# Casting q and early k in the loading DMA, bundling the attention work of a step, a two-input mask and layer-norm applies on VectorE, in a fused sliding-window attention and gMLP kernel

## The chip, the cores and the metric

One core of one Trainium2 chip runs the kernel. The metric is the device time of one execution in microseconds (us). Engines are named as in the profile: PE is TensorE, PEld its weight loads, DVE is VectorE, ACT is ScalarE, POOL is GpSimd, SP is SyncE. "L311" is line 311 of the kernel file of that run.

## The reference, cut to what matters

```python
# attention: 8 batches, 8 heads, 576 positions, head size 64, window of 64 positions
scores = scale * q @ k.transpose(0, 1, 3, 2)
mask = (rel >= 0) & (rel < 64)               # rel = query position - key position
attn = softmax(where(mask, scores, -1e9))
x = (attn @ v) -> [8, 576, 512]              # heads side by side

# gMLP on x
h = relu(x @ w_in);  u, v = h[..., :512], h[..., 512:]
v_n = (v - mean(v)) / sqrt(var(v) + 1e-6)    # layer norm without gain
v_s = einsum('ts,bsd->btd', w_spatial, v_n) + b_spatial[None, :, None]
out = (u * v_s) @ w_out                      # float32
```

## The kernel before

Each batch's attention is five steps: four pairs of heads, and one step for the last 64 positions of all heads. A step has these pieces: T (transposes of q and k on TensorE, then a copy `qk` on VectorE), S (scores), E (exponential on ScalarE, then the mask on VectorE), P (a product with ones for the softmax sums, then the products with v), N1 (logarithm of the sums) and N2 (reciprocal, then VectorE's `x`). The gMLP of the batch before supplies products V, U, G and O. `oz`, the PSUM tile of P, has one buffer, so the P of a step waits until VectorE has made `x` of the step before. The gMLP products share three PSUM buffers called `mm`.

```python
# loads: f32, by hardware queues; q, and k of the first three batches, in 1 KB runs
def load_runs(b, x, h0, n, eng):
    eng.dma_start(NAT[b][x] ... [:, h0:h0 + n, :],
                  SRC[x][b, h0:h0 + n, 0:512, :].rearrange("h (p j) d -> p h (j d)", j=4))

# casts to f16: one per tensor and head pair, on GpSimd (batch 0: k on ScalarE, q on VectorE)
steps.append([lambda p=p: cast_pair(b, 1, p, engk), lambda p=p: cast_pair(b, 0, p, engq),
              lambda p=p: cast_pair(b, 2, p, nc.gpsimd), lambda p=p: shift_pair(b, p, nc.gpsimd)])

# T: 8 transposes of 128 columns; E: the mask
for c in range(4):
    nc.tensor.transpose(tp[:, 128 * c:128 * c + 128], Qh[:, c, 2 * s:2 * s + 2, :], id16[:, :])
nc.vector.scalar_tensor_tensor(e2[:, :, :], e2[:, :, :], 0.0, m, ALU.max, ALU.min)

# layer norm of batch b
nc.vector.scalar_tensor_tensor(nb[:, :], mv[:, :, 0], -1.0, rs[:, :], ALU.mult, ALU.mult)
for j in range(5):
    ...
    (nc.vector if b < 1 else nc.gpsimd).tensor_scalar(
        vn[0:jn, :], vs[0:jn, :], rs[0:jn, j:j + 1], nb[0:jn, j:j + 1], ALU.mult, ALU.add)

# one step: gMLP products (todo) are put between the pieces
def att_step(i, s, todo, before, between, nxt):
    if nxt is not None:
        emit_T(*nxt)
    run(todo, before)
    post = []
    if i < B:
        emit_S(i, s)
        post.append(lambda: emit_E(i, s))
    if state["P"] is not None:
        pb, ps_ = state["P"]
        emit_P(pb, ps_)
        post.append(lambda: emit_N1(pb, ps_))
        post.append(lambda: emit_N2(pb, ps_))
    while post:
        post.pop(0)()
        run(todo, between)
    state["P"] = (i, s) if i < B else None
```

The softmax here doesn't subtract the row's maximum and nothing guards it: scores larger than these inputs give would overflow.

## Time and profile before

The median is 262.28 us (261.06 to 264.21, three runs); in the profiled execution the span is 259.1 us. Busy time of each engine, from the top of the profile page, and engines' shares of the chain of waits that ended last:

```profile
PE 220.0 (85%) x2586; PEld 117.0 (45%) x2586; DVE 165.8 (64%) x298; ACT 152.3 (59%) x272; POOL 172.8 (67%) x275
...
PE 52%; POOL 12%; DVE 12%; ACT 12%; DMA 5%; issue 5%; ACTq 1%; POOLq 0%; SPq 0%
```

TensorE is the busiest, but half of the chain runs through other engines. The next rows cut the span at three products: the first V product, the second batch's fourth U product (U4, where the chain of waits enters it), and the same product five batches later. A row gives the window, its length, the busy time of PE, PEld, DVE, ACT and POOL (with instruction counts), the granted TensorE clock, the busy share of the DMA queues (packets overlap, so it can exceed 1) and GB/s. The last row is one steady batch.

```profile
0.00:32.00 32.00, 23.49 (x251) 11.91 (x251) 19.49 (x49) 13.23 (x22) 25.09 (x46) 0.89 1.10 230
32.00:91.56 59.56, 45.82 (x506) 24.96 (x502) 39.44 (x69) 32.75 (x58) 45.06 (x80) 0.86 1.02 233
91.56:223.90 132.34, 121.20 (x1571) 66.01 (x1570) 93.39 (x155) 89.26 (x160) 98.84 (x147) 1.00 0.49 127
223.90:259.10 35.20, 29.50 (x266) 14.13 (x263) 13.50 (x26) 17.09 (x32) 3.77 (x5) 1.00 0.19 68
...
145.70:171.86 26.16, 24.25 (x316) 13.24 (x314) 18.87 (x31) 17.84 (x32) 22.06 (x34) 1.00 0.73 182
```

In the first two rows, 91.56 us, TensorE is idle for 22 us (91.56 − 23.49 − 45.82) and the clock is below full. In a steady batch it is idle for 1.9 of 26.16 us. The timeline of TensorE shows where. Its columns are the start, the duration, the instruction, and in brackets the idle time before it with what ended it:

```profile
165.88 0.41 PE L311 MATMUL oz_1_3167<-e_5_1_3067,onesK 128*64 128x512 f16 x2 [1.07 <-DVE x_0_3101 L339]
...
170.72 0.39 PE L430 MATMUL ps_0_3240<-wspT_153,vn_3_3137 128*128 128x512 f16 x1 [0.36 <-POOL vn_3_3137 L400]
171.47 0.39 PE L430 MATMUL ps_0_3240<-wspT_154,vn_0_137 65*128 65x512 f16 x1 [0.36 <-POOL vn_0_137 L400]
```

The ones product waits for `x`, and the first G product waits for layer-norm outputs that GpSimd makes one after another. Before the steady state, four waits stand out in the list of waits of 45 to 93 us (total, times, longest):

```profile
POOL hv_784 L119 <- DMA nv_608<-in_v_dram: 7.7, 1, 7.7
...
PE oz_3_1198 L311 <- DVE x_2_1159 L339: 6.0, 1, 6.0
PEld L238 <- POOL hk_783 L119: 4.5, 1, 4.5
...
ACT ob_3_1152 L455 <- DMA out_dram<-ob_0_1059: 3.3, 1, 3.3
```

ScalarE stands 3.3 us before an output copy because an output buffer is still being stored, and TensorE's 6.0 us follow.

### The profile page before, as it was taken

Reading aid. Unit: us, or ns where it says so; the run is one execution under the profiler, and the core shown is the slowest. Engines: PE = TensorE matmul, PEld = TensorE weight load, DVE = VectorE, ACT = ScalarE, POOL = GpSimd, SP = SyncE. Lnnn points to the kernel's source line nnn. Section 1 sums busy time; section 2 is a strip of 40 time slices with the busy share of each in tenths; the row PEclk is TensorE's granted clock in tenths of the full one; section 3 lists DMA queues with packets and bytes.
Section 4 is the critical chain, followed back from the end, with each engine's and each line's share of the span. In section 5 each row is a group of like instructions: output and inputs, shape, how many; then the busy total and the mean of one; then the engine's idle time right before and its main releaser. Section 6 shows DMA issues by size and latency. Waiting matters only on the chain.

```text
span 259.1 us, 6474 instructions
## 1 busy us (share of the span) xinstructions
PE 220.0 (85%) x2586; PEld 117.0 (45%) x2586; DVE 165.8 (64%) x298; ACT 152.3 (59%) x272; POOL 172.8 (67%) x275
## 2 busy tenths in 40 slices
PE   8577895899097899868998899889988998899892
PEld 2344452455054355534554455446543654354350
DVE  2866676485389556964878387838783878376130
ACT  3344575147357646774588558855885488657422
POOL 2799979129979995969688968897789402400500
PEclk9959999599779799999999999999999999999999
DMA  7999999999999809990587858680220023002304
GB/s 194 293 220 242 210 262 243 237 204 259 256 223 253 184 4 226 265 240 3 121 238 199 177 123 227 194 193 0 83 101 4 3 81 105 1 3 81 104 11 171
DMA packets 85310, 40.41 MB, mean 156 GB/s; under 512 B 68192, under 2 KB 80032, under 8 KB 85280
## 3 DMA queue, kind: packets, MB, share of 16 engines
q1 hardware_dynamic: 80448, 34.87, 56.1%
q0 software_dynamic: 1408, 2.24, 4.6%
q10 hardware_dynamic: 3424, 2.88, 3.5%
q8 instruction: 20, 0.33, 0.5%
q14 instruction: 10, 0.08, 0.1%
HBM read 32.79 MB, written 9.44 MB: 163 GB/s over the span
## 4 chain that ended last, share of the span: by engine, by line
PE 52%; POOL 12%; DVE 12%; ACT 12%; DMA 5%; issue 5%; ACTq 1%; POOLq 0%; SPq 0%
DMA out_dram<-ob_0_1059 3%; DMA nq_78<-in_q_dram 2%; POOL vn_1_138 L400 1%; DMA out_dram<-ob_1_4740 1%; POOL vn_0_137 L400 1%; PE ps_0_810 L430 1%; DVE maskr L194 1%; PE warm_304 L158 1%; POOL vn_1_2013 L400 1%; PE pv_0_1260 L364 1%; POOL vn_1_4201 L400 1%; POOL vn_1_3679 L400 1%; POOL vn_1_3133 L400 1%; POOL vn_1_2573 L400 1%; POOL vn_0_1460 L400 1%
## 5 line engine op out<-in xcount | busy, mean ns | idle before, releaser
L311 PEld LDWEIGHTS <-onesK 128*64 128x64 f16 x80 | 6.0, 107 | 19.5 <-issue 16.9
L400 POOL TENSOR_SCALAR vn_0_4595<-vs_0_4520,rs_4590,nb_4591 128x512 f16<-128x512 f16 x1 | 0.8, 773 | 17.3 <-PE pu_0_4613 L410 17.3
L400 POOL TENSOR_SCALAR vn_0_4199<-vs_0_4051,rs_4194,nb_4195 128x512 f16<-128x512 f16 x1 | 0.8, 772 | 14.7 <-DVE nb_4195 L392 14.7
L119 POOL CAST hv_102<-nv_80 128x512 f16<-128x512 f32 (+1 forms) x5 | 5.0, 997 | 5.4 <-DMA nv_80<-in_v_dram 5.3
L158 PEld LDWEIGHTS <-scratch 128*128 128x128 f16 x49 | 5.0, 117 | 7.3 <-issue 4.1
L119 POOL CAST hv_784<-nv_608 128x512 f16<-128x512 f32 (+1 forms) x5 | 3.1, 613 | 7.7 <-DMA nv_608<-in_v_dram 7.7
L158 PE MATMUL warm_105<-scratch 128*128 128x512 f16 x14 | 5.9, 616 | 1.3 <-DVE scratch L153 1.3
L119 POOL CAST hq_782<-nq_606 128x256 f16<-128x256 f32 (+1 forms) x9 | 4.6, 533 | 2.3 <-DMA nq_606<-in_q_dram 2.3
L119 POOL CAST hk_1232<-nk_794 128x512 f16<-128x512 f32 (+1 forms) x5 | 5.7, 1131 | 0.2
L311 PE MATMUL oz_3_1198<-e_1_3_1143,onesK 128*64 128x512 f16 x2 | 0.6, 608 | 6.0 <-DVE x_2_1159 L339 6.0
L294 ACT ACTIVATE e_1_0_837<-sc_0_819 128x1024 f16<-128x1024 f32 x1 | 1.0, 1024 | 7.6 <-PE sc_0_819 L273 7.6
L137 POOL COPY hs_1761<-hv_1760 64x512 f16<-64x512 f16 x4 | 3.3, 828 | 3.0 <-PE oz_4_1822 L324 2.8
L117 ACT CAST hk_101<-nk_79 128x256 f16<-128x256 f32 x8 | 2.8, 400 | 3.9 <-DMA nk_79<-in_k_dram 3.9
L410 PEld LDWEIGHTS <-win_141 128*128 128x128 f16 x32 | 3.2, 101 | 4.1 <-issue 0.6
L410 PEld LDWEIGHTS <-win_142 128*128 128x128 f16 x32 | 3.2, 101 | 4.1 <-issue 0.6
L119 POOL CAST hk_2319<-nk_1763 128x512 f16<-128x512 f32 (+1 forms) x5 | 4.8, 961 | 0.2
L119 POOL CAST hk_3439<-nk_2883 128x512 f16<-128x512 f32 (+1 forms) x5 | 4.8, 961 | 0.2
L119 POOL CAST hk_2879<-nk_2323 128x512 f16<-128x512 f32 (+1 forms) x5 | 4.8, 961 | 0.2
L119 POOL CAST hk_417<-nk_421 128x256 f16<-128x256 f32 (+1 forms) x9 | 4.5, 527 | 0.3
L119 DVE CAST hq_100<-nq_78 128x256 f16<-128x256 f32 x8 | 2.1, 300 | 4.0 <-DMA nq_78<-in_q_dram 4.0
L119 POOL CAST hq_1758<-nq_1235 128x256 f16<-128x256 f32 (+1 forms) x9 | 4.6, 531 | 0.0
L410 PEld LDWEIGHTS <-win_140 128*128 128x128 f16 x32 | 3.3, 102 | 2.9 <-issue 0.3
(1869 smaller groups left out, 1000.7 us busy)
## 6 DMA issues: line engine op xcount, KB each, us to landing
nv_422<-in_v_dram SPq DMA_DIRECT2D x9, 128.0 KB, 5.0
nk_79<-in_k_dram SPq DMA_DIRECT2D x4, 256.0 KB, 4.9
nq_78<-in_q_dram SPq DMA_DIRECT2D x4, 256.0 KB, 4.8
nk_421<-in_k_dram SPq DMA_DIRECT2D x4, 256.0 KB, 8.2
nq_420<-in_q_dram SPq DMA_DIRECT2D x4, 256.0 KB, 8.7
nk_607<-in_k_dram SPq DMA_DIRECT2D x2, 512.0 KB, 5.8
nq_606<-in_q_dram SPq DMA_DIRECT2D x2, 512.0 KB, 8.6
nv_608<-in_v_dram SPq DMA_DIRECT2D x4, 256.0 KB, 7.3
```

What stands on the lines that cost most here:

```text
L117: nc.scalar.copy(o, i)
L119: eng.tensor_copy(o, i)
L137: eng.tensor_copy(vs[0:64, 0:4, hs, :], vn[0:64, 0:4, hs, :])
L158: nc.tensor.matmul(t[:, :], scratch[:, 0:128], scratch[:, :], start=True, stop=True)
L194: nc.vector.tensor_scalar(maskr[:, u, :], keep[:], -1.0, BIG, ALU.mult, ALU.add)
L294: nc.scalar.activation(e2[:, :, :], sc[:, :, :], AF.Exp, bias=0.0, scale=0.125)
L311: nc.tensor.matmul(oz[64 * h:64 * h + 64, 1, 0:n], onesK[:, :], e2[:, h, 0:n], start=True, stop=True)
L364: nc.tensor.matmul(pv[:, :], X[b, r][:, 128 * j:128 * j + 128], w_in_sb[r][:, 512:1024], start=(r == 0), stop=(r == 3))
L400: (nc.vector if b < 1 else nc.gpsimd).tensor_scalar(vn[0:jn, :], vs[0:jn, :], rs[0:jn, j:j + 1], nb[0:jn, j:j + 1], ALU.mult, ALU.add)
L410: nc.tensor.matmul(pu[:, :], w_in_sb[r][:, 128 * m:128 * m + 128], X[b, r][:, :], start=(r == 0), stop=(r == 3))
L430: nc.tensor.matmul(ps[:, :], VN[b, kk][0:kn, 128 * m:128 * m + 128], wspT[kk][0:kn, 0:512], start=(kk == 0), stop=(kk == 4))
```

## The change

The intent is to take work off GpSimd and to take the two steady waits away. It has these parts.

1. **Loads.** q, and k of the first three batches, are loaded by GpSimd's DMA queue, which casts to f16 on the way. Their casts go, and q's f32 tiles. The v shift copies read f32.
2. **Half-width transposes.** The casting loads leave each head's 1 KB run together, so q and early k are transposed 64 columns at a time: sixteen instead of eight transposes.
3. **Mask.** A two-input `min` in place of `max` then `min`.
4. **Bundle.** P, S, N1, T, E, N2 of a step are issued together, and its gMLP products after them.
5. **Layer-norm applies** of all batches on VectorE, as subtract then multiply.
6. **Output buffers**: five instead of three, all stores by SyncE.

```diff
-    def load_runs(b, x, h0, n, eng):
-        eng.dma_start(NAT[b][x][:, 0:4, :, :] ...
+    def load_runs(b, x, h0, n):
+        nc.gpsimd.dma_start(runs(b, x)[:, h0:h0 + n, :, :].rearrange("p h j d -> p h (j d)"),
+                            SRC[x][b, h0:h0 + n, 0:512, :].rearrange("h (p j) d -> p h (j d)", j=4))
 # ... (start of the program: six of ten casting loads here, the mask source "keep" after all ten)
+    for p in (2, 3):
+        for x in (1, 0):
+            load_runs(0, x, 2 * p, 2)
+    for x in (1, 0):
+        load_runs_rem(0, x)
 # ... (emit_T)
+                    for j in range(4):
+                        for h in (0, 1):
+                            nc.tensor.transpose(tp[64 * h:64 * h + 64, o + 128 * j:o + 128 * j + 128],
+                                                src[:, 2 * s + h, j, :], id16[:, :])
 # ... (emit_E)
-        nc.vector.scalar_tensor_tensor(e2[:, :, :], e2[:, :, :], 0.0, m, ALU.max, ALU.min)
+        nc.vector.tensor_tensor(e2[:, :, :], e2[:, :, :], m, ALU.min)
 # ... (emit_LN)
-            (nc.vector if b < 1 else nc.gpsimd).tensor_scalar(
-                vn[0:jn, :], vs[0:jn, :], rs[0:jn, j:j + 1], nb[0:jn, j:j + 1], ALU.mult, ALU.add)
+            nc.vector.tensor_scalar(vn[0:jn, :], vs[0:jn, :], mv[0:jn, j, 0:1],
+                                    rs[0:jn, j:j + 1], ALU.subtract, ALU.mult)
 # ... (outputs)
-        ob = mpool.tile([128, 512], f32, tag="ob", bufs=3, name=f"ob{b}_{j}")
+        ob = mpool.tile([128, 512], f32, tag="ob", bufs=5, name=f"ob{b}_{j}")
 # ... (one step)
-    def att_step(i, s, todo, before, between, nxt):
+    def att_step(i, s, nxt):
+        if state["P"] is not None:
+            emit_P(*state["P"])
+        if i < B:
+            emit_S(i, s)
+        if state["P"] is not None:
+            emit_N1(*state["P"])
         if nxt is not None:
             emit_T(*nxt)
-        # ... interleaved pieces and products
+        if i < B:
+            emit_E(i, s)
+        if state["P"] is not None:
+            emit_N2(*state["P"])
         state["P"] = (i, s) if i < B else None
 # ... (second batch)
-        att_step(1, s, todo, 1, 1 if s else 0, (1, s + 1) if s < 4 else (2, 0))
+        att_step(1, s, (1, s + 1) if s < 4 else (2, 0))
+        run(todo, 3 if s < 3 else 1)
```

## The prediction

> **What bounds it now.** From 93 to 250 us TensorE: the table of stages has it busy 24.2 us of each 26.2 us batch, at full clock. Its timeline for 145.7-171.9 us shows two real gaps per batch: 1.1 us before the ones-product of head pair 1 (waiting for VectorE's x_0, which frees the single oz buffer) and about 1.1 us inside the first gate product, waiting for layer-norm outputs from GpSimd (four applies of 0.75 us, one of 1.7). The first 93 us are not TensorE-bound: the DMA row reads nine tenths, GpSimd is busy 20.4 of 21 us between 10 and 31 us, and the list of waits has ScalarE held 3.3 us by the first output store, TensorE 6.0 us behind that, 4.5 us for a k cast, GpSimd 7.7 us for v. In the tail the last layer-norm leaves TensorE idle about 4.2 us (chain of waits, 240.7-244.9).
>
> **What the change does.**
> - Removed: q casts on GpSimd (3-4 us a batch), early k casts (3-4), layer-norm applies there (4.8), batch 0's k and q casts on ScalarE and VectorE (5 in all).
> - Mask: a 1.2-1.6 us scalar_tensor_tensor becomes a tensor_tensor. The Trainium skill, "VectorE: DVE Perf Modes" (mode table), allows a 16-bit tensor_tensor two results a cycle; no trace shows it yet. Estimate 0.7 us.
> - Moved: five applies to VectorE at 0.2-0.7 us each (batch 0's took 0.7-1.1 there beside busy GpSimd). VectorE stays near 18 us a batch.
> - Added: 176 transposes, by halving widths. The P products show two 64-column halves starting every 0.03 us, so about nothing on TensorE.
> - Added: casting loads on GpSimd's queue. The Trainium skill, "DMA: Bandwidth & Descriptors" (SWDGE vs HWDGE), says only that queue casts and GpSimd's cores write the descriptors. The trace has 0.53-0.56 us for up to 128 rows; these have 256 or 512 runs. Estimate: 1.0 and 1.6 us.
> - Moved: P, S, N1, T, E, N2 as one bundle, then products; P's inputs are a step old. Output buffers: three to five.
>
> **Critical path.**
> 1. Start: slower. The mask source is now built behind ten casting loads on GpSimd, and VectorE builds the masks before it copies the first qk. First exponential from 9.6 to about 17 us; steps of batch 0 from about 5 to 4.3 us. First V product from 32 to 37 us: +5.
> 2. Second attention (47.6-73.2 us), no store stall: -6.
> 3. Next iteration up to its fourth U product (91.6 us), no waits for casts, warmer clock: -5.
> 4. Five steady periods, 132 us together, each to about 24.3: -11.
> 5. Tail, applies on VectorE with GpSimd idle: -3.
>
> Sum -20, with 1 us more or less for rounding: 262.3 to **241 us**, range 232 to 251. Chances: over 2% faster 0.93, within 2% 0.05, slower 0.02.
>
> **What would show it.** Steady period 24.0-24.7 us between fourth U products, no wait of the ones-product on x or of the first gate product on vn; GpSimd busy under 16 us a batch; mask op near 0.7 us; a head pair's transposes within 0.5 us; no ScalarE wait on an output store; first exponential later than 9.6 us; casting-load instructions of 0.6-2 us; last layer-norm gap under 2 us.
>
> **What would make it wrong.** Casting loads costing GpSimd much more than 1.6 us, or held by VectorE, delaying masks and v casts (start +10 or more); casting runs that move slowly and starve batches 1 and 2; half-transposes that don't run as pairs (+1.2 us a batch); evictions on ScalarE queued behind the bundle, so that three product buffers stall TensorE; the applies blocking the next qk copy or mask. If casting loads cost only 0.55 us, the start is even and the time nears 235.

## The result

The changed kernel takes 237.81 us (median of four runs, 236.10 to 239.86) beside 262.4 us for the kernel before. The ratio is 0.904, with a 95% interval of 0.892 to 0.915. A ratio here is the mean time of one kernel's fast runs over that of the other's in the same rounds, so it is not quite the ratio of the medians. (The record calls a run slow when it is more than 1.5% above the fastest of the same kernel, and leaves it out.)

The four runs fall on two levels, 236.1 us (twice) and 239.5 to 239.9 us. The first profile caught the upper one (239.86 us, span 238.1 us); a later profile of the same file caught the lower one (span 234.0 us, run e5 below), a fast run. Both are shown, and the fast one is to be compared with the profile before, which is of a fast run too. The page of the second:

```profile
PE 213.8 (91%) x2762; PEld 116.1 (50%) x2762; DVE 154.2 (66%) x317; ACT 149.1 (64%) x264; POOL 114.2 (49%) x186
...
PE 76%; DVE 10%; ACT 6%; POOL 3%; issue 3%; POOLq 0%; ACTq 0%
```

GpSimd's busy time fell by 59 us, and three quarters of the chain is now TensorE. The same cuts of the span as before, first profile, with a steady batch last:

```profile
0.00:33.73 33.73, 23.41 (x284) 11.46 (x284) 15.57 (x41) 10.22 (x14) 28.07 (x51) 0.90 1.22 189
33.73:84.62 50.89, 44.47 (x602) 24.70 (x600) 35.88 (x73) 34.03 (x61) 33.26 (x52) 0.93 1.02 180
84.62:206.28 121.66, 121.66 (x1651) 67.41 (x1650) 89.37 (x176) 89.39 (x160) 52.60 (x83) 1.00 0.63 132
206.28:238.10 31.82, 27.87 (x231) 13.72 (x229) 14.38 (x30) 15.35 (x30) 0.00 (x0) 0.99 0.22 75
...
133.28:157.61 24.33, 24.33 (x331) 13.47 (x330) 18.01 (x36) 17.91 (x33) 13.31 (x21) 1.00 0.83 169
```

and the second profile:

```profile
0.00:33.79 33.79, 22.49 (x284) 11.34 (x285) 15.86 (x41) 10.33 (x14) 27.93 (x51) 0.90 1.21 186
33.79:80.52 46.73, 41.74 (x602) 23.62 (x600) 34.59 (x73) 34.03 (x61) 33.69 (x53) 1.00 1.14 199
80.52:202.17 121.65, 121.65 (x1651) 67.40 (x1650) 89.37 (x176) 89.37 (x160) 52.60 (x83) 1.00 0.64 131
202.17:234.00 31.83, 27.88 (x232) 13.71 (x229) 14.40 (x30) 15.36 (x30) 0.00 (x0) 0.98 0.23 75
```

TensorE is busy for all of five steady batches: neither wait is left. The start is slower, and everything else is shorter. The two profiles differ in the second row alone, by 4.2 us: TensorE is busy 2.7 us longer there, at a lower clock (0.93 and 1.00), and idle 1.4 us longer. The timeline of TensorE and one window of each show how that comes about. First profile:

```profile
47.48 0.64 PE L272 MATMUL sc_0_778<-qk_0_767 64*64 64x128 f16 x16 [3.41 <-DVE qk_0_767 L255]
...
48.00:52.00 4.00, 4.00 (x30) 1.86 (x24) 2.21 (x4) 1.02 (x1) 3.75 (x7) 0.50 1.42 182
```

Second profile, at the same instruction:

```profile
46.09 0.42 PE L272 MATMUL sc<-qk 64*64 64x128 f16 x16 [1.99 <-DVE qk L255]
...
48.00:52.00 4.00, 4.00 (x73) 2.34 (x71) 2.54 (x5) 1.76 (x3) 3.75 (x6) 1.00 1.33 179
```

Ahead of that `qk` copy VectorE makes the five applies of batch 0. In the first profile they took 0.69 to 0.82 us each, in the second 2.02 us for all five. GpSimd issues the same loads and makes the same casts beside them in both, so why they took longer in the first is not shown. The gap in TensorE's work was 3.41 and 1.99 us, and only with the longer one was the clock granted 0.50. The Trainium skill, "TensorE: Matmul & The Clock Gate" (What's actually happening), says that the clock halves after about one idle window of 3.4 us, in windows that run free of the kernel. These two profiles fit that, but the experiments below, at the same instruction, fit it only in part. After a gap of 2.09 us (e7) the clock stayed at 1.00. After 2.86 us (e4) and 3.11 us (e8), both shorter than such a window, it fell (means of 0.75 and 0.64 over a window of 4 us). After 2.82 us (e12) and 3.52 us (e9) it stayed at 1.00 for the next 16 us:

```profile
45.05 0.42 PE L273 MATMUL sc<-qk 64*64 64x128 f16 x16 [3.52 <-DVE qk L247]
...
45.00:61.00 16.00, 14.31 (x222) 8.70 (x222) 11.89 (x18) 9.23 (x15) 7.78 (x15) 1.00 1.10 233
```

So the length of the gap alone does not decide whether the clock falls. No experiment here shortened the gap alone, so this cause of the two levels is read from profiles and not tested.

### The profile page after: what moved, and what is told of

Same layout as the page of the kernel before. It is cut to its first block, busy times and chain, and to the rows that moved or that the text cites. A ratio compares the mean times of both kernels' runs of the same rounds, so it can differ in the third digit from the quotient of the medians.

```text
span 238.1 us, 6631 instructions
## 1 busy us (share of the span) xinstructions
PE 217.4 (91%) x2762; PEld 117.3 (49%) x2762; DVE 155.2 (65%) x317; ACT 149.0 (63%) x264; POOL 113.9 (48%) x186
## 3 DMA queue, kind: packets, MB, share of 16 engines
HBM read 32.79 MB, written 9.44 MB: 177 GB/s over the span
## 4 chain that ended last, share of the span: by engine, by line
PE 78%; DVE 9%; ACT 6%; POOL 3%; issue 3%; POOLq 0%; ACTq 0%
POOL hk_79 L78 1%; POOL hq_78 L78 1%; PE ps_0_820 L427 1%; PE warm_222 L143 1%; PE pu_3_829 L407 1%; PE warm_257 L143 1%; DVE mask L184 1%; DVE mask L186 1%; PE ps_1_837 L427 1%; PE ps_0_4383 L427 0%; PE ps_0_3855 L427 0%; PE ps_0_3304 L427 0%; PE ps_0_2741 L427 0%; PE ps_0_2178 L427 0%; PE ps_2_4476 L427 0%
## 5 line engine op out<-in xcount | busy, mean ns | idle before, releaser
L310 PEld LDWEIGHTS <-onesK 128*64 128x64 f16 x80 | 5.2, 107 | 16.7 <-issue 13.3
L293 ACT ACTIVATE e_0_0_218<-sc_0_200 128x1024 f16<-128x1024 f32 x1 | 1.0, 1024 | 12.7 <-PE sc_0_200 L272 12.7
L112 POOL CAST hk_1226<-nk_775 128x512 f16<-128x512 f32 x4 | 2.8, 695 | 10.2 <-PE tp_4_1120 L248 10.0
L186 DVE TENSOR_SCALAR mask<-keep 128x64 f16<-128x64 f16 x4 | 1.5, 384 | 8.6 <-POOL keep L175 8.6
L272 PE MATMUL sc_0_200<-qk_0_184 64*64 64x128 f16 (+2 forms) x16 | 0.6, 306 | 7.0 <-DVE qk_0_184 L255 7.0
L143 PE MATMUL warm_95<-scratch 128*128 128x512 f16 x14 | 5.3, 556 | 1.3 <-DVE scratch L138 1.3
L407 PEld LDWEIGHTS <-win_137 128*128 128x128 f16 x32 | 3.2, 99 | 4.0 <-issue 0.3
L407 PEld LDWEIGHTS <-win_138 128*128 128x128 f16 x32 | 3.2, 99 | 3.9 <-issue 0.3
L407 PEld LDWEIGHTS <-win_135 128*128 128x128 f16 x32 | 3.2, 100 | 3.7 <-issue 0.3
L407 PEld LDWEIGHTS <-win_136 128*128 128x128 f16 x32 | 3.2, 100 | 3.7 <-issue 0.3
L112 POOL CAST hv_1227<-nv_961 128x512 f16<-128x512 f32 x4 | 2.4, 612 | 4.7 <-DMA nv_961<-in_v_dram 4.7
L112 POOL CAST hv_3458<-nv_3126 128x512 f16<-128x512 f32 x4 | 2.4, 612 | 4.5 <-PE tp_0_3392 L244 4.5
L117 POOL CAST hs_1770<-nv_1441 64x512 f16<-64x512 f32 x4 | 2.9, 724 | 3.4 <-PE oz_4_1780 L323 3.4
L117 POOL CAST hs_2333<-nv_2000 64x512 f16<-64x512 f32 x4 | 2.9, 724 | 3.2 <-PE oz_4_2343 L323 3.2
L117 POOL CAST hs_2896<-nv_2563 64x512 f16<-64x512 f32 x4 | 2.9, 724 | 3.1 <-PE oz_4_2906 L323 3.1
L112 POOL CAST hv_1769<-nv_1441 128x512 f16<-128x512 f32 x4 | 2.4, 612 | 4.0 <-PE oz_3_1663 L323 4.0
L112 POOL CAST hk_2894<-nk_2340 128x512 f16<-128x512 f32 x4 | 2.5, 636 | 3.8 <-PE tp_4_2722 L248 3.6
L112 POOL CAST hk_2331<-nk_1777 128x512 f16<-128x512 f32 x4 | 2.5, 636 | 3.8 <-PE tp_4_2159 L248 3.6
L112 POOL CAST hk_3457<-nk_2903 128x512 f16<-128x512 f32 x4 | 2.5, 636 | 3.8 <-PE tp_4_3285 L248 3.6
L112 POOL CAST hv_2895<-nv_2563 128x512 f16<-128x512 f32 x4 | 2.4, 612 | 3.8 <-PE sc_4_2809 L285 3.8
L112 POOL CAST hv_2332<-nv_2000 128x512 f16<-128x512 f32 x4 | 2.4, 612 | 3.7 <-PE sc_4_2246 L285 3.7
## 6 DMA issues: line engine op xcount, KB each, us to landing
nk_775<-in_k_dram SPq DMA_DIRECT2D x4, 256.0 KB, 10.7
```

Of the source, the lines that this page charges most:

```text
L112: nc.gpsimd.tensor_copy(F16[b, x][:, 0:4, hs, :], NAT[b, x][:, 0:4, hs, :])
L117: nc.gpsimd.tensor_copy(vs[0:64, 0:4, hs, :], vf[0:64, 0:4, hs, :])
L143: nc.tensor.matmul(t[:, :], scratch[:, 0:128], scratch[:, :], start=True, stop=True)
L186: nc.vector.tensor_scalar(mask[:, 0, :, u, :], kview, -1.0, BIG, ALU.mult, ALU.add)
L272: nc.tensor.matmul(jp(sc[r:r + 64, h, :])[:, :, p0:p1], qk[d, 512 + 64 * kap:576 + 64 * kap], jp(qk[d, 0:512])[:, :, p0:p1], start=True, s ...
L293: nc.scalar.activation(e2[:, :, :], sc[:, :, :], AF.Exp, bias=0.0, scale=0.125)
```

## The experiments

All runs gave a correct result. Ratios are to the kernel before, timed on the same chip in the same rounds. e1 to e4 shared one chip, e5 to e8 another, e9 to e11 a third, and e12 had a fourth; across chips, only ratios are compared. "First V" is the start of the first V product; "U4" and the period are as above.

| run | what it is | median us | ratio (95% interval) |
|---|---|---|---|
| e1 | after, old interleaving | 247.73 | 0.948 (0.942 to 0.955) |
| e2 | after, applies on GpSimd, new form | 305.71 | 1.173 (1.163 to 1.183) |
| e3 | after, old mask op | 246.94 | 0.946 (0.939 to 0.953) |
| e4 | after, mask source first | 233.97 | 0.897 (0.890 to 0.903) |
| e5 | after, again | 238.10 | 0.909 (0.903 to 0.914) |
| e6 | after, applies on GpSimd, old form | 251.03 | 0.960 (0.956 to 0.965) |
| e7 | before + bundle, applies, mask op | 235.44 | 0.901 (0.896 to 0.905) |
| e8 | after, start and second attention repaired | 232.86 | 0.891 (0.888 to 0.895) |
| e9 | before + bundle | 264.90 | 1.017 (1.010 to 1.024) |
| e10 | before + applies on VectorE | 255.56 | 0.978 (0.969 to 0.988) |
| e11 | e7 with the repairs of e8 | 235.50 | 0.903 (0.895 to 0.911) |
| e12 | before + bundle + applies on VectorE | 243.79 | 0.932 (0.928 to 0.937) |

The theory was the prediction's: the bundle removes the wait for `x`, the applies on VectorE remove the wait for `vn`, the cheaper mask op pays for the applies on VectorE, and the casting loads and output buffers make the second and third batches shorter and the start longer. The main rival was that the loads, the headline of the change, are what matters, or that one of the other parts does it all.

### e1: the bundle undone

```diff
-                att_step(i, s, nxt)
+                att_step(i, s, st[s], 2, 1, nxt)      # and the old att_step
```

> The changed kernel with the old interleaving of attention pieces and products put back. My theory: the bundle is what removed the wait of the ones-product on x_0, so it comes back at about 1.1 us a steady batch, and the second attention lengthens by 1-2 us: time about 245 us (ratio to before 0.93-0.94), steady period about 25.3 us with a wait of the ones-product on x in it. Rival (relief of GpSimd by the casting loads explains the gain): at most 2 us slower than the changed kernel, period 24.3-24.6 us.

Measured: 247.73 us. The period is 25.49 us, and TensorE waits for `x` again, for 7.7 us in eight places over the run:

```profile
PE oz L310 <- DVE x L338: 7.7, 8, 1.7
```

By ratio it lies 4 to 4.5 points above the changed kernel (0.948 against 0.904 and 0.909), or some 10 to 12 us of 262. The bundle is worth that much when everything else is in place.

### e2 and e6: the applies back on GpSimd

```diff
-            nc.vector.tensor_scalar(vn[0:jn, :], vs[0:jn, :], mv[0:jn, j, 0:1],
+            (nc.vector if b < 1 else nc.gpsimd).tensor_scalar(vn[0:jn, :], vs[0:jn, :], mv[0:jn, j, 0:1],
```

> The changed kernel with the layer-norm applies of batches 1 to 7 back on GpSimd. If the move to VectorE closed the wait inside the first gate product, it returns at about 1.1 us a batch plus 3 us in the tail: +9 us, about 246. Rival: the bundle alone gives the applies an earlier start, and GpSimd freed of q casts is quick enough: period grows by under 0.5 us, only the tail loses 2-3 us: about 240-241. I lean to the rival, +4 us, because the applies' results are first needed 3 us after rs is ready.

Both expectations missed by far: 305.71 us. The timeline of GpSimd in e2 shows five applies in 10.51 us, 2.1 us each:

```profile
144.87 10.51 POOL L397 TENSOR_SCALAR vn<-vs,mv,rs 128x512 f16<-128x512 f16 x5 [4.31 <-issue]
```

In the kernel before the same engine took 0.77 us for an apply, but in the form multiply then add. So e2 changed the arithmetic form on GpSimd too (and the operand, the mean from `mv`), and is no fair undo. It was done again with the old form:

```diff
-            nc.vector.tensor_scalar(... mv[0:jn, j, 0:1], rs[0:jn, j:j + 1], ALU.subtract, ALU.mult)
+            (nc.vector if b < 1 else nc.gpsimd).tensor_scalar(
+                vn[0:jn, :], vs[0:jn, :], rs[0:jn, j:j + 1], nb[0:jn, j:j + 1], ALU.mult, ALU.add)
```

> The applies of batches 1 to 7 back on GpSimd, now in the old form (multiply by rs, add nb; 0.75 us each in the kernel before), because in the subtract-then-multiply form each took 2.1 us there and the run e2 measured that. Theory that the move itself closed the wait in the first gate product: five applies of 0.75 us are 2 us longer than five of 0.4 on VectorE, so G0 waits 0.5-1.5 us a batch and 2-3 us in the tail: +5 to +10 us. Rival (bundle gave them room, GpSimd is free): +2 to +3 us, tail alone. I expect +4: about 242.

Measured: 251.03 us, 13 us more than e5 in the same rounds, and the expectation of about 4 missed as well. The timelines of GpSimd and VectorE in e6 show a second cost:

```profile
156.83 3.78 POOL L399 TENSOR_SCALAR vn<-vs,rs,nb 128x512 f16<-128x512 f16 x5 [4.77 <-DVE nb L391]
```

```profile
160.13 2.70 DVE L299 TENSOR_TENSOR e<-e,mask 128x1024 f16<-128x1024 f16 x1 [0.44 <-ACT e L293]
162.75 0.68 DVE L338 TENSOR_TENSOR x<-oz,zi 128x512 f16<-128x512 f32 x1
163.35 1.27 DVE L432 TENSOR_TENSOR g<-ps,ru 128x512 f16<-128x512 f32 x2
```

The mask op takes 2.70 us, where another in the same batch takes 0.69 us. It starts beside the last apply and ends during the casts that follow it on GpSimd without a pause. Four mask ops of the run took 2.64 to 2.70 us. VectorE's `x` and `g` come behind it, and TensorE then waits for `g` (4.3 us in four waits over the run) beside the wait for `vn` (4.4 us in eleven). Between 85 and 230 us it is 4.3 us for `g` and only 1.8 us for `vn`, so in the steady batches most of the listed loss comes by way of VectorE. The Trainium skill, "SBUF — State Buffer" (Who interferes with whom), says that a VectorE instruction with two SBUF inputs contends with a GpSimd instruction that reads SBUF, and that the one which comes second is blocked. This trace agrees that they contend, 2.70 against 0.69 us, but the mask op was held beyond the apply in front of it, which ended at 160.61 us. The period is 26.2 us, as in the kernel before, though every other part of the change is there.

### e3: the old mask op

```diff
-        nc.vector.tensor_tensor(e2[:, :, :], e2[:, :, :], m, ALU.min)
+        nc.vector.scalar_tensor_tensor(e2[:, :, :], e2[:, :, :], 0.0, m, ALU.max, ALU.min)
```

> The changed kernel with the scalar_tensor_tensor mask back (1.2-1.6 us in place of 0.7). VectorE has 6 us of slack in a steady batch, so the period stays 24.3-24.5; the steps of batch 0 and of the second attention, which are chains through ScalarE and VectorE, lengthen by 0.5 us each: +3 to +4 us, about 240.5. Rival (VectorE speed carries the steady gain): period over 25 us, +8 us.

Measured: 246.94 us, by ratio some 4 points or 10 us above the changed kernel and more of a loss than expected. The period is 24.73 us, with a 0.3 us wait for `g` in each batch. Beside the first profile of the changed kernel (spans 244.8 and 238.1 us), 2 us are lost over five periods, 2.5 up to the first V product (36.29 us in place of 33.73), and about 2 between that and U4. Beside the second, which is of a fast run as e3's is, about 5.8 us are lost between the first V product and U4; in e3 the clock fell there too (0.72 from 50 to 56 us, after a gap of 2.94 us), so that part is not the mask op's own time alone. The mean of a mask op on a head pair is 0.81 us in e5.

### e4: the mask source ahead of the casting loads

```diff
+    keep = cpool.tile([128, 64], f16, name="keep")     # memset and two selects on GpSimd, moved up
     new_half(0, 0)
     ...
     for p in range(2):
         for x in (1, 0):
             load_runs(0, x, 2 * p, 2)
-    keep = ...
```

> The changed kernel with the mask source built on GpSimd before the casting loads of batch 0 instead of after them. My theory of the late start (first exponential 14.8 us, VectorE waiting 8.6 us for the mask source): masks are built by 6 us, the first exponential comes at 9-10 us, all later stages move forward: 232-234 us, ratio 0.885-0.89. Rival (the start is limited by the arrival of q, k or v or by GpSimd's total work): under 2 us gained.

Measured: 233.97 us. The first exponential starts at 9.44 us and the first V product at 29.83, where the changed kernel has 14.77 and 33.73. The changed kernel's start, from its timelines of GpSimd, VectorE and ScalarE in turn, was this:

```profile
1.29 0.83 POOL L78 DMA_DIRECT2D hk_79<-in_k_dram  x1 [0.79 <-POOLq L598]
2.13 0.72 POOL L78 DMA_DIRECT2D hq_78<-in_q_dram  x1
...
9.59 0.24 POOL L175 TENSOR_SCALAR_AFFINE_SELECT keep<-keep 128x64 f16<-128x64 f16 x1
...
9.87 0.57 DVE L186 TENSOR_SCALAR mask<-keep 128x64 f16<-128x64 f16 x1 [8.59 <-POOL keep L175]
...
14.77 1.02 ACT L293 ACTIVATE e_0_0_218<-sc_0_200 128x1024 f16<-128x1024 f32 x1 [12.69 <-PE sc_0_200 L272]
```

Ten casting loads of about 0.72 us each fill GpSimd up to 9 us, `keep` comes behind them, and VectorE builds the mask (up to 13 us) before it copies the first `qk`. Moving three instructions takes that away, so the slow start was the order of issue and not the speed of the loads.

### e5: the changed kernel again

> The changed kernel unaltered, as the yardstick on the same chip as the next three: 236 to 240 us, ratio 0.90-0.91, in two levels 3 us apart as before.

Measured: 238.10 us (235.59 to 239.68 in six runs), ratio 0.909 against 0.904 of the first measurement. The range is the same, but the six runs (235.6, 235.8, 237.7, 238.5, 238.6 and 239.7) do not fall on two levels. Its profile is the second one above.

### e7: everything but the loads

The kernel before, with the bundle, the new mask op and the applies on VectorE. Its loads, casts, full-width transposes and three output buffers stay.

> The kernel before with the bundle, the applies on VectorE and the two-input mask, but its own loads, casts, full-width transposes and three output buffers. If the loads are worth little beyond what the bundle does: steady period 23.8-24.2 us (full-width transposes save 0.56 us a batch against the changed kernel), start 2 us earlier than before, the store stall of the second attention still there: about 243 us, ratio 0.925. Rival (GpSimd relief by casting loads is what frees TensorE): period above 25 us, ratio over 0.95.

Measured: 235.44 us, well under the 243 expected; ratio 0.901 against 0.909 for e5 in the same rounds. The intervals overlap slightly, so the kernel without the loads is as fast as the one with them, or a little faster. The windows of the first batch after U4, in which GpSimd still catches up, and of a steady one:

```profile
82.02:107.72 25.70, 24.78 (x318) 13.56 (x317) 20.08 (x36) 17.79 (x32) 24.57 (x44) 1.00 1.12 251
131.60:155.50 23.90, 23.90 (x316) 13.36 (x314) 19.16 (x36) 17.88 (x33) 15.96 (x29) 1.00 0.83 191
```

The steady period is 23.90 us, 0.43 shorter than in the changed kernel. Here TensorE has no half-width transposes. GpSimd, with its q casts, is busy 24.57 of 25.70 us in one batch, where it catches up, but it isn't late afterwards. The longest wait of ScalarE on an output store is 0.7 us, with three buffers. The rival that the loads are what matters is gone.

This is a balance of gains and losses. In the profiles the first V product comes at 30.28 us (33.79 in e5), the stretch from there to U4 takes 51.74 us (46.73), and the rest nearly the same. e7 leaves out the loads, the half widths and the output buffers at once, and its profile is of the slowest of its six runs (237.57 us). In it TensorE stands still for 3.2 us in the second attention, and the clock falls:

```profile
60.02 0.64 PE L311 MATMUL oz<-e,onesK 128*64 128x512 f16 x2 [3.19 <-DVE x L339]
...
60.00:68.00 8.00, 7.46 (x84) 4.79 (x84) 3.28 (x7) 3.90 (x7) 7.66 (x17) 0.50 0.97 257
```

Ahead of that wait ScalarE, which issues some of the stores here, begins to issue one 1.40 us after its copy was done, when a load of v has landed. In e5, where SyncE issues all stores, the wait for `x` at this place is 1.28 us and the clock stays at 1.00. So the loads, the buffers or the stores on SyncE are worth something there; no run separates them.

### e8: a better version

e4, with both masks built in the idle start, the last shift copy of batch 0 ahead of the casting loads of batch 1, the `w_spatial` transposes put between the V products, and the products of the second attention spread evenly.

```diff
     build_masks()
+    build_maskr()
     emit_T(0, 0)
 # ...
-    run(Vs_(0, range(4)))
-    emit_VO4(0, None)
     for kk in range(5):
+        if kk < 4:
+            emit_V(0, kk)
+        else:
+            emit_VO4(0, None)
         emit_W(kk)
 # ...
-        run(todo, 3 if s < 3 else 1)
+        run(todo, 3 if s < 1 else 2)
```

> An attempt to beat both: mask source before the casting loads as in e4, both masks built in the idle start, batch 0's last shift copy issued before batch 1's casting loads (e4 waited 1.6 us for it), the transposes of w_spatial interleaved with batch 0's V products, products of the second attention spread 3,2,2,2,2. Expected: 4 to 5 us for the start, 2.7 us for the interleaving, 1-2 us for the rest: about 229-231 us, ratio 0.875-0.885. If the start is limited by transfers instead, no better than e4 (234).

Measured: 232.86 us (231.15 to 233.86), ratio 0.891. It beats both kernels, though it falls short of the 229 to 231 us expected, and against e4 (0.897, on another chip) the intervals overlap, so what it adds to e4 is not shown. The first V product starts at 26.27 us and U4 of the second batch is at 77.42, 3.1 us ahead of e5. The period is 24.33 us, with TensorE busy throughout, so more is to be had only by less TensorE work, before 77 us, or in the tail, where TensorE is busy 27.88 of 31.83 us.

### e9, e10 and e12: the bundle and the applies, alone and together

e9 has the kernel before and the new `att_step`; e10 has the kernel before and the applies on VectorE in the old form; e12 has both, with the new form.

```diff
-            (nc.vector if b < 1 else nc.gpsimd).tensor_scalar(      # e10
+            nc.vector.tensor_scalar(
```

> The kernel before with the bundle alone. In e6 (bundle, applies on GpSimd) the steady period was 26.2 us, because GpSimd's applies held VectorE's mask op (2.7 us in place of 0.7) and so the gate multiplies and the product buffers. So alone the bundle should leave the steady period at 26-26.5 us and gain only in the second attention (about 5 us, e7 had no store wait there with three output buffers) and nothing in the tail: about 257 us, ratio 0.98. Rival (the parts add up): period 25 us, ratio 0.955.

> The kernel before with the applies on VectorE alone. e1 (everything but the bundle) had a period of 25.5 us with half-width transposes; here full-width ones save 0.4 but the mask op is the slow one: period 25.2-25.7, tail 3 us shorter, store stall still there: about 254 us, ratio 0.97. If move and bundle each need the other, the period stays at 26: ratio 0.985.

> The kernel before with the bundle and the applies on VectorE, but its old mask op, its own loads and three output buffers. Alone the bundle cost 1.7% and the applies gained 2.2%; if the two closed separate waits, both together would stand at about 260 us (ratio 0.995). My theory is that each alone only hands the wait to the other and that together they close it: ratio 0.93-0.945 (243-247 us), steady period 24.0-24.8 us, and the mask op then accounts for the rest of the way to e7 (0.90).

Measured: e9 is 1.7% slower than the kernel before (257 us were expected, 264.90 came), e10 2.2% faster, and e12 6.8% faster. The record calls e9 and e10 unclear, because their intervals reach to both sides of 2%; both exclude no change. The two parts alone add up to half a per cent. The list of waits of e9 for 85 to 230 us:

```profile
PE ps L430 <- POOL vn L400: 13.4, 11, 5.0
PE pu L410 <- ACT ob L455: 0.8, 1, 0.8
```

and of e10:

```profile
PE oz L311 <- DVE x L339: 8.1, 11, 2.0
```

In the same window of the kernel before, the listed waits add up to about 9.7 us for `x` and 4.6 for `vn`. With the bundle alone, TensorE waits for `x` no longer, but three times as long for GpSimd's `vn` (5.0 us of it in one wait at 87 us): the wait was handed on. With the applies alone, the wait for `vn` is gone, and that for `x` stays nearly whole. The windows of e12 show what the mask op adds:

```profile
137.18:162.48 25.30, 24.17 (x315) 13.28 (x314) 21.94 (x36) 17.92 (x32) 19.33 (x28) 1.00 0.76 186
...
187.22:211.47 24.25, 24.00 (x314) 13.36 (x314) 19.56 (x36) 17.93 (x32) 0.00 (x0) 1.00 0.15 50
```

While GpSimd works, e12's period is 25.3 us and VectorE is busy 21.94 of it; in the last batch, where GpSimd has nothing to do, the period is 24.25 us. The old mask op takes 1.33 us on average in e12. With the new one (e7, on another chip) the ratio is 0.901 in place of 0.932. My expectation of a period of 24.0 to 24.8 us for e12 held for its last two batches only.

### e11: the repairs of e8 with the old loads

> e7 (no casting loads, three output buffers) with e8's repairs of the start: both masks built in the idle start, w_spatial transposes between the V products, products of the second attention spread. If casting loads are worth nothing, it gains on e7 what e8 gained on e4 and lands at 231-233 us, equal to e8 (232.9). If they matter once the start is repaired, it stays at 235 or more, held by v casts on GpSimd and by transfers between 66 and 108 us.

Measured: 235.50 us, ratio 0.903, no gain over e7's 0.901. Here GpSimd's v casts wait for v:

```profile
POOL hv L119 <- DMA nv<-in_v_dram: 18.3, 5, 6.8
```

With the casting loads the repairs pay (e5 0.909, e8 0.891, in the same rounds), and the largest of them, the mask source put first, has no counterpart here. That they pay nothing without the casting loads is likely and not shown: e7 and e11 were timed on different chips, and so were e8 and e11, whose intervals just touch.

### A build that failed

Five output buffers in the kernel before do not fit: 43.4 kB were needed for them, with 39.8 kB left. The room in the changed kernel is that of the f32 tiles of q. Full-width transposes from the 1 KB-run layout do not build either: the build's message is that the stationary operand (the one held in the array) must have exactly one free dimension. That is why part 2 of the change exists. No run here separates parts 1 and 2.

## Why the prediction was right, point by point

The total was right: 241 us predicted, 237.81 measured, inside 232 to 251. That the total came so close is in part luck: the start was put 3 us too late, and the stretch after it gained about 2 us less (first profile) or more (second) than said. The table gives the sum by stages, with the first profile and the second (span 259.1 us before, 238.1 and 234.0 after; each term is the difference of the rows shown). The second compares fast with fast.

| stage | predicted | first profile | second profile |
|---|---|---|---|
| up to first V | +5 | +1.7 | +1.8 |
| first V to U4 of the second batch (terms 2 and 3) | −11 | −8.7 | −12.8 |
| five steady batches | −11 | −10.7 | −10.7 |
| tail | −3 | −3.4 | −3.4 |
| sum | −20 | −21.0 | −25.1 |

- **Steady batches: right, with two errors inside.** The period was predicted at about 24.3 us and is 24.33. Both waits are gone. But "about nothing on TensorE" for the half-width transposes is not right. The timeline of TensorE has a head pair's transposes in the kernel before from 149.00 to 149.44 us:

```profile
149.00 0.39 PE L238 MATMUL tp_0_2777<-id_120,hk_2319 128*128 128x128 f16 x4
149.22 0.39 PE L241 MATMUL tp_0_2777<-id_120,hq_2318 128*128 128x128 f16 x4
149.44 0.38 PE L430 MATMUL ps_2_2789<-wspT_150,vn_0_2571 128*128 128x512 f16 x1
```

  and in the changed one from 136.46 to 137.04, with only q in halves:

```profile
136.46 0.41 PE L240 MATMUL tp_0_2829<-id_110,hq_2338 128*64 128x128 f16 x8
136.81 0.40 PE L244 MATMUL tp_0_2829<-id_110,hk_2331 128*128 128x128 f16 x4
137.04 0.38 PE L427 MATMUL ps_2_2852<-wspT_146,vn_0_2633 128*128 128x512 f16 x1
```

  That is 0.58 against 0.44 us, 0.14 us a pair and 0.56 us a batch; the prediction had allowed 0.5 us for a pair. It is of the size of the 0.43 us by which e7's period is shorter. What the prediction lost here it won back elsewhere: it took 24.2 us of TensorE work a batch as given, but with full widths and no gap left a batch takes 23.90 us (e7). That the two errors cancelled is luck.

- **Start: right in direction, too large.** The step that failed is the issue cost of the casting loads, "1.0 and 1.6 us". They cost 0.70 to 0.83 us, with 256 or 512 runs alike. The first exponential came at 14.77 us and not 17, and the first V at +1.7 and not +5. The reason was named correctly: `keep` behind ten casting loads. e4 shows it, and removes it.

- **Terms 2 and 3: right in sum, the causes right only in part.** "No store stall: −6" and "no waits for casts: −5" credited the output buffers and the loads. e7 has neither, and its stretch from the first V product to U4 takes 51.74 us, 7.8 less than before; the changed kernel's is 8.7 and 12.8 less. e7's longest store wait is 0.7 us with three buffers. So most of the gain is that of the bundle, the applies and the mask op together, and which of the three moves the stores out of ScalarE's way there, I did not take apart. The 0.9 to 5.0 us left may be the loads', the stores' or the clock's, which fell in e7's profile and in the first one; that stays open.

- **Tail: right in size, wrong reading behind it.** The prediction said that the last layer-norm leaves TensorE idle about 4.2 us, from the chain of waits. The chain only says that GpSimd's applies were the last thing to end. The window shows TensorE busy 3.28 of these 4.25 us:

```profile
240.70:244.95 4.25, 3.28 (x14) 1.19 (x13) 0.00 (x0) 1.78 (x4) 3.77 (x5) 1.00 0.42 140
```

  so about 1 us of idle time was to be won. TensorE's idle time in the tail fell by 1.7 us (35.20 − 29.50 against 31.82 − 27.87). The rest of the 3.4 us is work: 35 fewer matmuls lie behind the cut (266 and 231), and most of them are attention products, which the bundle puts ahead of the product at which I cut.

- **Mask op: right.** In e5, 20 of 32 took 0.67 to 0.69 us and the others, made beside GpSimd's casts, 0.85 to 1.12; the mean is 0.81. The Trainium skill, "VectorE: DVE Perf Modes" (the perf-mode tier table), gives a 16-bit `tensor_tensor` two results a cycle. The trace agrees: 0.69 us for 1024 elements against 1.2 to 1.6 us for the old op in the kernel before.

- **Other marks.** GpSimd is busy 13.3 us a batch (predicted under 16), the applies take 0.40 us each on VectorE in the steady state, the last layer-norm leaves no listed wait on TensorE, and no wait of ScalarE on an output store is listed.

- **What the prediction did not see**: that the parts are worth far more together than alone. It added them up by stages, and that sum came out; a sum by parts would not have (e9 +1.7%, e10 −2.2%, both −6.8%, with the mask op −9.9%). And the loads, the first thing named in the change, add nothing on balance as built.

## What to carry to other kernels

When an engine waits at two places in one period, a change that removes one of them may only move the time to the other. Test such parts together as well as alone, and judge each by undoing it in the full version. Before you credit the headline of a change, build the version that has everything but it. Work that a new DMA queue's issuing engine must do first belongs ahead of the loads in that engine's order, and a chain of waits that runs through an engine does not say that the bottleneck was idle meanwhile: look at that engine's own window.

## What the Trainium skill lacked or had wrong

- "DMA: Bandwidth & Descriptors" (Anatomy of one DMA) calls descriptor generation "small, variable", says that many can be emitted before the extra cost shows, and gives no figure for how long one load occupies GpSimd. In these traces a casting load on its queue occupies it for 0.70 to 0.83 us, with 256 or 512 runs, and the loads of up to 128 rows in the kernel before for 0.53 to 0.77 us. So the time hardly grows with the count, as the page says, but it is not small: ten loads in a row cost 7 us.
- "GPSIMD Engine Reference" (3.1 Elementwise) has 769 ns for 512 elements in a tight loop, and the multiply-then-add `tensor_scalar` of this kernel agrees with 0.77 us. No page says that the form of a `tensor_scalar` matters there: subtract then multiply, with the mean read from `mv`, took 2.1 us on GpSimd for the same tile (e2), and 0.40 us on VectorE. The runs do not separate the operations from the operand.
- "SBUF — State Buffer" (Who interferes with whom) was right about a two-input VectorE op beside a reading GpSimd. It does not say that such an op can be held beyond the GpSimd instruction in front of it: GpSimd went from instruction to instruction with hardly a pause, and one mask op took 2.70 us in place of 0.69 (e6), ending 2.2 us after the apply beside which it started.
- "TensorE: Matmul & The Clock Gate" (Part 3, Packing small matmuls) gives packed tiles of one array an issue cost of a few nanoseconds. Eight half-width transposes of 128x64 here took 0.35 us up to the next instruction where four full-width ones took 0.22 us: halving the width of a transpose was not free.
- The same page (What's actually happening) lets the clock fall after an idle window of about 3.4 us. Here it fell after a gap of 2.86 us (e4) and stayed at 1.00 after one of 3.52 us (e9).
